# Which engines cut x into its two fp32r terms: ScalarE, VectorE and GpSimd by turns, or ScalarE and GpSimd alone

## The chip, the cores and the metric

The kernel runs on one core of a Trainium2 chip. The core has a matrix engine (TensorE), three engines for elementwise work (VectorE, ScalarE, GpSimd), an engine that issues transfers (SyncE) and DMA queues. Each engine works through its own list of instructions in order, and semaphores tie the lists together. The metric is device time in microseconds of one execution of the whole program. The profile is of one such execution: it gives each instruction's start, its duration, and what ended the idle time in front of it.

In the profile PE stands for TensorE's matmuls, PEld for its weight loads, DVE for VectorE, ACT for ScalarE, POOL for GpSimd and SP for SyncE.

## What is computed

Attention with a sliding window of 128 positions and a distance bias, and behind it a feed-forward layer:

```python
scores = scale * np.matmul(q, k.transpose(0, 1, 3, 2))       # 8 batches, 8 heads, 576 x 64
scores = np.where(mask, scores + bias[None], -1000000000.0)  # 0 <= row - column < 128
...
attn = np.exp(scores)
attn = attn / (np.sum(attn, axis=-1, keepdims=True) + 1e-09)
return np.matmul(attn, v).astype(np.float32)
...
x = np.ascontiguousarray(attn_out.transpose(0, 2, 1, 3)).reshape(B * S, H * D)   # 4608 x 512
h = x @ w_in                                                 # 512 x 2048
g = h * (1.0 / (1.0 + np.exp(-1.702 * h)))
return (g @ w_out).astype(np.float32)                        # 2048 x 512
```

Everything is float32. The matmuls of the feed-forward layer run in a reduced format, fp32r. To keep the precision, an operand a is cut into two fp32r terms, a rounded one (ah) and what is left (al = a - ah), and a product is made of three: ah bh + ah bl + al bh.

## The kernel before

The attention's output x is kept transposed, in chunks of T = 256 rows of the 4608, each a tile `xf` of 128 partitions x 4 quarters x 256 columns. There are 18 chunks. Chunks 0 to 11 are computed by objects of the class `Job`, one chunk each; chunk 0 is done in two jobs, for the first 8 blocks of 128 hidden columns and for the other 8, so there are 13 jobs. Chunks 12 to 17 are computed two at a time by objects of the class `Pair`, in another scheme of products, which does not use the function that is changed.

A job first calls `split_x` (L560), which makes the tiles `xh` (L564, rounding, as the cast of a copy) and `xl` (L566, subtraction), quarter by quarter: 4 roundings and 4 subtractions of 128x256 each. Rounding is on ScalarE for the chunks in `BESIDE`, which are 0 to 3 (5 jobs), and on VectorE for chunks 4 to 11 (8 jobs). The subtraction is on GpSimd for the even quarters and on VectorE for the odd ones. Both tiles have one buffer (the pool `xp` has bufs=1), so the split of the next job can write a tile only when the matmuls of the job before have read it.

Then, for each block f of 128 hidden columns, `Job.up(f)` (L580) runs 12 matmuls into `h_ps`, which has two buffers: 4 with `xh` and the weight's high term, 4 with `xh` and its low term, 4 with `xl` and the high term. Behind them come the tanh on ScalarE (L585), a product on VectorE that gives `g` (L586), its rounding on ScalarE (`gh`, L589) and the subtraction on GpSimd (`gl`, L590). `Job.down(f)` (L600) runs 6 matmuls of 512 columns into `acc`: two with each of `gh` and the two weight terms, and the last two with `gl`. The main loop over all blocks of all jobs calls, in each step, the decoding of weights that are still to come, the attention's ticks (`advance`), then `up` of the next block (through `begin`, with the split, if it is the first of a job), then `down` of this one.

The attention's units run beside it, in ticks. On GpSimd these have the subtractions for Q, K and V (L329, L330, L318), a sum (L551), and, in the first two batches, the normalisation `pb` (L420), for which the transposes of L438 wait. On ScalarE they have the roundings (L310, L328, L317), the exponentials (L399) and copies out of PSUM (L474, L548). In the first part of the program the weights come in and are decoded and cut too, on all three engines (L227 to L233), and sums of them are made and stored (L654 to L665).

The program's order is not the order of the source alone: the program is built with `schedule_with_timeline_sim=True`, so a planner lays out each engine's list by a timeline of its own when the program is built. On the chip each list then runs in that order.

Of the kernel before, what the change touches and what calls it, by code (L numbers as in the profile page):

```python
# [8 lines left out]
F32 = mybir.dt.float32  # L9
# [5 lines left out]
ALU = mybir.AluOpType  # L15
# [18 lines left out]
BIG = 3.0e38  # L34
FAR = 1.0e37
DEPTH = 3
BESIDE = range(4)
WB = 2
DECODE_TICKS = 5, 6, 7
FETCH_AHEAD = 6  # L40
# [113 lines left out]
def tile_kernel(ctx: ExitStack, tc: tile.TileContext, q0, k0, v0, qT, kT, v, w_in, w_out, out):  # L154
    nc = tc.nc
# [404 lines left out]
    def split_x(c, x):  # L560
        xh = xp.tile([P, NC, T], F32R, name="xh")
        xl = xp.tile([P, NC, T], F32R, name="xl")
        for k in range(NC):
            (nc.scalar.copy if c in BESIDE else nc.vector.tensor_copy)(xh[:, k], x[:, k])  # L564
            sub = nc.vector if k % 2 else nc.gpsimd
            sub.tensor_tensor(xl[:, k], x[:, k], xh[:, k].bitcast(F32), ALU.subtract)  # L566
        return xh, xl

    class Job:
# [330 lines left out]
    def begin(j):  # L900
        nonlocal seen
        recall(j.c)
        x = xf.pop(j.c)
        j.xh, j.xl = split_x(j.c, x)
        if j.f1 < NF:
            xf[j.c] = x
            send(j.c)
        seen = max(seen, j.c)
        recall(seen + 1)
        j.up(j.f0)  # L910
# [130 lines left out]
```

## Time and profile before

| | |
|---|---|
| time, median of 3 runs | 1059.15 us (1058.39 to 1060.15) |
| time of the profiled execution | 1062.32 us |
| its span, first to last instruction | 1060.5 us |
| mean granted TensorE clock | 0.988 of full speed |
| DMA traffic | 151.91 MB, 143 GB/s on average |
| the splits of x start at | 16, 89, 152, 186, 254, 313, 377, 439, 499, 562, 622, 684 and 744 us |

The span is what the profile's shares refer to. Matmuls are pipelined and their ends are modelled, so the start of one stands about 0.115 us (256 columns) behind the last although each is given as 0.28. A row of a timeline has the start, the time from the start to the end of a run of equal instructions, the engine, the line, the operation, output and inputs, the shapes, and the number of instructions. In square brackets stand the idle time before it and what ended that. A row of a view by groups has the number of instructions, their busy time, the mean time of one, and the idle time of the engine in front of them with what ended most of it.

### The profile page before, as it was taken

Reading aid. Unit: us, or ns where it says so; the run is one execution under the profiler, and the core shown is the slowest. Engines: PE = TensorE matmul, PEld = TensorE weight load, DVE = VectorE, ACT = ScalarE, POOL = GpSimd, SP = SyncE. Lnnn points to the kernel's source line nnn. Section 1 sums busy time; section 2 is a strip of 40 time slices with the busy share of each in tenths; the row PEclk is TensorE's granted clock in tenths of the full one; section 3 lists DMA queues with packets and bytes.
Section 4 is the critical chain, followed back from the end, with each engine's and each line's share of the span. In section 5 each row is a group of like instructions: output and inputs, shape, how many; then the busy total and the mean of one; then the engine's idle time right before and its main releaser. Section 6 shows DMA issues by size and latency. Waiting matters only on the chain.

```text
span 1060.5 us, 21877 instructions
## 1 busy us (share of the span) xinstructions
PE 1037.9 (98%) x6897; PEld 913.6 (86%) x6897; DVE 683.0 (64%) x2280; ACT 675.4 (64%) x1974; POOL 620.1 (58%) x832
## 2 busy tenths in 40 slices
PE   8889999999999999999999999999999999999998
PEld 5557878789998999999899999999988998898987
DVE  6877576357777787867778686776744345436343
ACT  6968876568777777777777777777633334335332
POOL 3668887457676677767677676766642233215121
PEclk9969999999999999999999999999999999999999
DMA  8975456333224234332423432342174556556551
GB/s 286 371 239 185 147 160 196 108 85 94 80 83 131 82 96 125 112 80 89 141 83 113 119 107 81 106 136 69 57 274 163 170 174 212 179 165 205 188 179 60
DMA packets 120276, 151.91 MB, mean 143 GB/s; under 512 B 40033, under 2 KB 96865, under 8 KB 120161
## 3 DMA queue, kind: packets, MB, share of 16 engines
q1 hardware_dynamic: 114400, 140.55, 42.6%
q10 hardware_dynamic: 5760, 9.96, 2.6%
q8 instruction: 55, 0.90, 0.4%
q14 instruction: 61, 0.49, 0.2%
HBM read 119.01 MB, written 31.46 MB: 142 GB/s over the span
## 4 chain that ended last, share of the span: by engine, by line
PE 79%; DVE 4%; issue 1%; DMA 1%; ACT 1%; POOL 0%; POOLq 0%; ACTq 0%; SPq 0%; DVEq 0%
PE acc L600 21%; PE h_ps L580 21%; PE accs L780 11%; PE X_ps L721 6%; PE s_ps L352 5%; PE x_ps L518 4%; PE Y_ps L721 4%; PE t_ps L461 4%; PE x_ps L495 1%; DVE xf L710 0%; DMA xf<-x 0%; PE t_ps L438 0%; DVE xh L564 0%; DMA part<-wc 0%; DVE xl L566 0%
## 5 line engine op out<-in xcount | busy, mean ns | idle before, releaser
L580 PE MATMUL h_ps<-xh,w 128*128 128x256 f32 x1536 | 251.5, 288 | 8.4 <-DVE g L586 7.5
L580 PEld LDWEIGHTS h_ps<-xh,w 128*128 128x128 f32 x1536 | 213.4, 190 | 26.9 <-issue 7.5
L600 PE MATMUL acc<-w,gh 128*128 128x512 f32 x768 | 220.8, 402 | 0.5 <-ACT g L585 0.4
L590 POOL TENSOR_TENSOR gl<-g,gh 128x256 fp32r<-128x256 f32 x192 | 147.1, 767 | 99.4 <-ACT gh L589 78.0
L733 POOL TENSOR_TENSOR gs<-g,gs 128x512 fp32r<-128x512 f32 x48 | 63.4, 1320 | 168.7 <-PE Y_ps L721 113.8
L780 PE MATMUL accs<-w,gs 128*128 128x512 f32 x576 | 148.3, 393 | 0.3 <-POOL gs L733 0.3
L600 PEld LDWEIGHTS acc<-w,gh 128*128 128x128 f32 x768 | 131.7, 190 | 18.2 <-ACT g L585 0.8
L330 POOL TENSOR_TENSOR K<-rk,K 128x384 fp32r<-128x384 f32 (+1 forms) x120 | 108.8, 907 | 50.7 <-ACT K L328 45.5
L580 PE MATMUL h_ps<-xl,w 128*128 128x256 f32 x768 | 137.2, 284 | 0.2 <-DVE xl L566 0.2
L600 PE MATMUL acc<-w,gl 128*128 128x512 f32 x384 | 127.3, 407 | 1.1 <-POOL gl L590 1.1
L780 PEld LDWEIGHTS accs<-w,gs 128*128 128x128 f32 x576 | 102.2, 189 | 17.7 <-POOL gs L733 0.7
L580 PEld LDWEIGHTS h_ps<-xl,w 128*128 128x128 f32 x768 | 112.4, 191 | 5.2 <-issue 0.6
L399 ACT ACTIVATE pb<-pb,mins 128x256 f32<-128x256 f32 (+2 forms) x216 | 104.6, 486 | 11.6 <-DVE mins L380 11.1
L586 DVE SCALAR_TENSOR_TENSOR g<-g,h_ps 128x256 f32<-128x256 f32 x192 | 79.5, 415 | 49.6 <-ACT g L585 48.1
L589 ACT CAST gh<-g 128x256 fp32r<-128x256 f32 x192 | 77.6, 405 | 50.2 <-DVE g L586 45.4
L585 ACT ACTIVATE g<-h_ps 128x256 f32<-128x256 f32 x192 | 72.7, 380 | 56.1 <-PE h_ps L580 45.9
L380 DVE CUSTOM_DVE_ANT_0 pb<-s_ps,bias 128x256 f32<-128x256 f32 (+3 forms) x240 | 86.0, 380 | 26.9 <-PE s_ps L352 24.7
L424 DVE TENSOR_SCALAR_CACHE_REDUCE pb<-pb,rec 128x256 f32<-128x256 f32 (+2 forms) x216 | 91.0, 454 | 3.2
L329 POOL TENSOR_TENSOR Q<-rq,Q 64x256 fp32r<-64x256 f32 (+1 forms) x120 | 83.0, 691 | 13.6 <-ACT Q L310 3.4
L480 DVE TENSOR_TENSOR pl<-t_ps,ph 128x512 fp32r<-128x512 f32 (+2 forms) x120 | 72.9, 607 | 16.0 <-ACT ph L474 14.1
L461 PE MATMUL t_ps<-ident,pb 128*128 128x128 f32 x408 | 80.8, 272 | 0.5 <-DVE pl L480 0.5
L328 ACT CAST K<-rk 128x384 fp32r<-128x384 f32 (+1 forms) x120 | 56.5, 471 | 29.4 <-PE s_ps L352 23.7
(116 smaller groups left out, 2057.8 us busy)
## 6 DMA issues: line engine op xcount, KB each, us to landing
ring<-part SPq DMA_DIRECT2D x84, 512.0 KB, 3.3
rk<-kT SPq DMA_DIRECT2D x72, 192.0 KB, 2.6
rq<-qT SPq DMA_DIRECT2D x96, 128.0 KB, 2.4
out<-o ACTq DMA_DIRECT2D x34, 256.0 KB, 2.8
rw<-w_in SPq DMA_DIRECT2D x16, 512.0 KB, 6.0
rw<-w_out SPq DMA_DIRECT2D x16, 512.0 KB, 6.8
x<-xf SPq DMA_DIRECT2D x13, 512.0 KB, 3.4
xf<-x SPq DMA_DIRECT2D x13, 512.0 KB, 4.4
```

Source lines behind the costliest of these rows:

```text
L329: nc.gpsimd.tensor_tensor(Q[D:], rq[D:], Q[D:].bitcast(F32), ALU.subtract)
L330: nc.gpsimd.tensor_tensor(K2, rk, K1.bitcast(F32), ALU.subtract)
L380: nc.vector.tensor_tensor_reduce(b.p[ra:rb, cs:b.end], u.s[ra:rb, e, cs:b.end], bias[head][ra:rb, cs:b.end], -SCALE, BIG, ALU.add, ALU.min ...
L399: nc.scalar.activation(live, live, AF.Exp, bias=u.mins[:b.rows, e:e + 1], scale=-1.0, accum_out=u.sums[:b.rows, e, :1],)
L424: nc.vector.tensor_scalar(live, live, u.rec[:rows, e:e + 1], None, ALU.mult, ALU.add, u.rec[:rows, 2 + e:3 + e])
L461: nc.tensor.transpose(u.t[:c.n, w:w + b.rows], b.p[:b.rows, col:col + c.n], ident[:b.rows, :b.rows])
L580: nc.tensor.matmul(h, w1[f][:, z, k * P:(k + 1) * P], x[:, k], start=(n == 0), stop=(n == len(ops) - 1))
L586: nc.vector.scalar_tensor_tensor(g, g, 1.0, h, ALU.add, ALU.mult)
L590: nc.gpsimd.tensor_tensor(gl, g, gh.bitcast(F32), ALU.subtract)
L600: products.append(nc.tensor.matmul(acc, g[:, t * P:(t + 1) * P], w2[f][:, z], start=(f == self.f0 and n == 0), stop=(f == self.f1 - 1 and ...
L721: nc.tensor.matmul(bank, w[:, z, k * P:(k + 1) * P], x[:, y, k], start=start and i == 0, stop=i == len(ops) - 1, skip_group_check=True)
L780: products.append(nc.tensor.matmul(self.acc[t], g[:, y, t * P:(t + 1) * P], w2[f][:, z], start=(f == 0 and n == 0), stop=(f == NF - 1 and ...
```

## The change

For every chunk, all four roundings are on ScalarE and all four subtractions on GpSimd. The five splits of chunks 0 to 3 (chunk 0 has two) had their roundings there already, so in these only the two odd subtractions move. In the eight splits of chunks 4 to 11 four roundings and two subtractions move.

```diff
-BESIDE = range(4)
...
         xh = xp.tile([P, NC, T], F32R, name="xh")
         xl = xp.tile([P, NC, T], F32R, name="xl")
         for k in range(NC):
-            (nc.scalar.copy if c in BESIDE else nc.vector.tensor_copy)(xh[:, k], x[:, k])
-            sub = nc.vector if k % 2 else nc.gpsimd
-            sub.tensor_tensor(xl[:, k], x[:, k], xh[:, k].bitcast(F32), ALU.subtract)
+            nc.scalar.copy(xh[:, k], x[:, k])
+            nc.gpsimd.tensor_tensor(xl[:, k], x[:, k], xh[:, k].bitcast(F32), ALU.subtract)
         return xh, xl
```

## What the change does to the time: the prediction

> **What bounds the kernel now.** I read the page first, then the busy time of stretches, then TensorE's own waits, then the two lines that change. The page, total and one group:
>
> ```profile
> span 1060.5 us, 21877 instructions
> ...
> PE 1037.9 (98%) x6897; PEld 913.6 (86%) x6897; DVE 683.0 (64%) x2280; ACT 675.4 (64%) x1974; POOL 620.1 (58%) x832
> ...
> L590 POOL TENSOR_TENSOR gl<-g,gh 128x256 fp32r<-128x256 f32 x192 | 147.1, 767 | 99.4 <-ACT gh L589 78.0
> ```
>
> TensorE is busy for 98% of the span and idle for 1060.5 - 1037.9 = 22.6 us. No other engine is above 64%. GpSimd mostly stands idle ahead of its most frequent job, `gl`, and waits there for ScalarE. But such shares are averages, so here are three stretches (busy us and instructions of each engine):
>
> ```profile
> core 0: us, PE busy (x) PEld busy (x) DVE busy (x) ACT busy (x) POOL busy (x), PEclk, DMA share, GB/s
> 16.00:89.00 73.00, 64.80 (x385) 44.30 (x383) 60.02 (x149) 54.66 (x162) 47.15 (x42) 0.86 0.91 313
> 89.00:100.00 11.00, 9.57 (x61) 7.79 (x60) 7.56 (x27) 9.35 (x31) 9.98 (x11) 1.00 0.22 73
> ...
> 313.00:745.00 432.00, 430.84 (x3028) 397.18 (x3027) 327.68 (x1347) 324.05 (x1001) 304.97 (x484) 1.00 0.36 104
> ```
>
> From 313 to 745 us, where eight of the thirteen splits of x lie (the last starts at its edge), TensorE is idle for 1.2 us of 432. There the three other engines have 24 to 29% of their time free. In the short stretch at 89 us, right behind the split of chunk 1, it is otherwise: GpSimd is busy for 9.98 of 11 us and TensorE loses 1.4. TensorE's waits, over the whole span (us, times, longest):
>
> ```profile
> PE h_ps L580 <- DVE g L586: 7.5, 4, 5.0
> PE t_ps L438 <- POOL pb L420: 2.9, 3, 1.9
> ...
> PE acc L600 <- POOL gl L590: 1.1, 1, 1.1
> ...
> PE h_ps L580 <- DVE xl L566: 0.2, 1, 0.2
> ```
>
> The split's own part in them is 0.2 us, once. So a quicker split has almost nothing to win directly, and the question is how much later the new one may be before TensorE feels it.
>
> **The change part by part.** The two lines, by form (count, busy us, mean ns, idle before), and then with least, median and longest ns:
>
> ```profile
> L566 POOL TENSOR_TENSOR xl<-xf,xh 128x256 fp32r<-128x256 f32 x26 | 21.4, 838 | 7.0 <-ACT xh L564 5.3 <-DVE xh L564 1.1 <-DVE rec L411 0.4
> ...
> L566 DVE TENSOR_TENSOR xl<-xf,xh 128x256 fp32r<-128x256 f32 x26 | 17.5, 691 | 1.0 <-ACT xh L564 0.8
> ...
> L564 DVE CAST xh<-xf 128x256 fp32r<-128x256 f32 x32 | 14.1, 495 | 1.2 <-PE h_ps L580 1.1
> ...
> L564 ACT CAST xh<-xf 128x256 fp32r<-128x256 f32 x20 | 6.9, 404 | 0.6 <-DVE xf L504 0.6
> ```
>
> ```profile
> L566 POOL TENSOR_TENSOR xl<-xf,xh x26: 726/839/975, 16.6 to 747.1; 128x256 fp32r<-128x256 f32 x26
> L566 DVE TENSOR_TENSOR xl<-xf,xh x26: 396/683/996, 20.4 to 746.6; 128x256 fp32r<-128x256 f32 x26
> ```
>
> ```profile
> L564 DVE CAST xh<-xf x32: 273/294/1241, 313.1 to 745.8; 128x256 fp32r<-128x256 f32 x32
> ...
> who waited for it (us, times):
> ...
>   PEld h_ps L580: 1.0, 2
> ```
>
> Load moves as follows. VectorE loses 32 roundings and 26 subtractions, 14.1 + 17.5 = 31.6 us. ScalarE gains 32 x 0.404 = 12.9 us. GpSimd gains 26 x 0.838 = 21.8 us, or 26 x 0.726 = 18.9 us if VectorE beside it no longer slows it. Nothing is issued to a DMA queue by these lines, and no number of bytes changes. The totals hide behind TensorE: GpSimd comes to 642 of 1060 us. What counts is the moment of each split.
>
> *Rounding, eight splits (chunks 4 to 11).* I look at the split at 377 us, the one with the least room:
>
> ```profile
> 378.11 0.46 POOL L318 TENSOR_TENSOR VV<-rv,VV 128x64 fp32r<-128x64 f32 x1
> 378.53 1.72 POOL L566 TENSOR_TENSOR xl<-xf,xh 128x256 fp32r<-128x256 f32 x2
> ...
> 383.57 0.74 POOL L590 TENSOR_TENSOR gl<-g,gh 128x256 fp32r<-128x256 f32 x1
> ```
>
> ```profile
> 377.14 1.58 DVE L564 CAST xh<-xf 128x256 fp32r<-128x256 f32 x4 [0.87 <-PE h_ps L580]
> ```
>
> ```profile
> 378.46 0.38 ACT L585 ACTIVATE g<-h_ps 128x256 f32<-128x256 f32 x1 [0.57 <-PE h_ps L580]
> ```
>
> ```profile
> 381.12 0.39 PE L580 MATMUL h_ps<-xl,w 128*128 128x256 f32 x2
> 381.38 0.49 PE L580 MATMUL h_ps<-xl,w 128*128 128x256 f32 x2
> ```
>
> ```profile
> 385.95 0.62 PE L600 MATMUL acc<-w,gl 128*128 128x512 f32 x2
> ```
>
> VectorE needs 1.58 us for the four roundings, and ScalarE took 1.32 us for four at 88.87 us (row below). ScalarE's queue gets up to 1.32 us in front of the tanh of L585. Behind that tanh stand `gh` (L589) and then GpSimd's `gl`. Here `gl` ends at 384.31 and is wanted at 385.95, which leaves 1.64 us, more than 1.32. VectorE's roundings stood in front of the same chain, at L586, and that delay goes. I take **0**. The gain cannot exceed the 1.0 us that weight loads waited for the roundings.
>
> *Subtraction, thirteen splits.* The two odd quarters now stand behind the two even ones in GpSimd's queue. With 0.84 us each, the last lands 1.68 us behind the present end of GpSimd's pair. At 377 us that is 378.53 + 1.72 + 1.68 = 381.93. TensorE takes the last quarter at 381.38 + 0.49 - 0.28 = 381.59 (0.28 being one matmul), so it would be 0.34 us late. The same sum for others, first and last of the thirteen among them:
>
> ```profile
> 30.66 0.40 DVE L566 TENSOR_TENSOR xl<-xf,xh 128x256 fp32r<-128x256 f32 x1
> 31.68 0.63 PE L580 MATMUL h_ps<-xl,w 128*128 128x256 f32 x4
> ```
>
> ```profile
> 88.87 1.32 ACT L564 CAST xh<-xf 128x256 fp32r<-128x256 f32 x4
> 89.35 1.81 POOL L566 TENSOR_TENSOR xl<-xf,xh 128x256 fp32r<-128x256 f32 x2 [0.88 <-ACT xh L564]
> ...
> 92.61 0.40 PE L580 MATMUL h_ps<-xl,w 128*128 128x256 f32 x2
> ```
>
> ```profile
> 684.57 1.57 POOL L566 TENSOR_TENSOR xl<-xf,xh 128x256 fp32r<-128x256 f32 x2 [0.50 <-DVE xh L564]
> ...
> 687.77 0.50 PE L580 MATMUL h_ps<-xl,w 128*128 128x256 f32 x3
> ```
>
> ```profile
> 746.26 1.79 POOL L566 TENSOR_TENSOR xl<-xf,xh 128x256 fp32r<-128x256 f32 x2
> ...
> 750.03 0.40 PE L580 MATMUL h_ps<-xl,w 128*128 128x256 f32 x2
> ```
>
> The first split gets x quarter by quarter, so its last subtraction merely takes 0.73 instead of 0.40 us: 31.39 against 31.68. At 89 us the landing is 92.84 against 92.73, 0.11 late. At 684 us it is 687.82 against 687.99, in time, and at 746 us 749.73 against 750.15, in time. Eleven of thirteen come in time in this way. The sum of what is late is 0.34 + 0.11, about **+0.5 us**.
>
> Behind these subtractions GpSimd's other jobs wait 1.5 us longer. At 377 us `gl` comes 3.3 us after the pair and has the 1.64 us of room. In the long stretch I take 0 for this. The full stretch at 89 us is another matter:
>
> ```profile
> 93.47 2.01 POOL L420 TENSOR_SCALAR pb<-pb,rec 128x128 f32<-128x128 f32 x2
> 96.02 1.52 POOL L420 TENSOR_SCALAR pb<-pb,rec 128x128 f32<-128x128 f32 x2 [0.54 <-ACT wh L660]
> ```
>
> Four subtractions alone, 4 x 0.73 = 2.9 us, replace a pair of 1.81: GpSimd gets 1.1 us more where 1.0 is free, and these `pb` rows are what the transposes of L438 wait for. Between 0 and +1.1 us I take the middle, **+0.5 us**.
>
> The Trainium skill, "GPSIMD Engine Reference", Engine selection, speaks against the move: two-input elementwise work belongs on VectorE, GpSimd being about twice as slow. The trace's least times agree, 726 against 396 ns. If that price fell on the path, the sum would be up to 26 x 0.33 = 8.6 us; rival B is its form here.
>
> **Sum:** 0 + 0.5 + 0.5 = +1.0 us. The profiled execution took 1062.3 us, 1.8 outside its span, and lies 3.2 above the median of 1059.15. Carried to the median, the forecast is **1060.2 us**. A difference under 0.2% (2.1 us) is about what a measurement of this kernel cannot tell from none, so I call this no change.
>
> **The rivals.**
>
> *A, the forecast:* the extra delay stays inside the room that TensorE's order already leaves. Chance 0.50.
>
> *B, GpSimd turns late at each split (slower).* If a `gl` of 0.77 us gets between the four subtractions, the last lands 2.45 us behind the present pair's end instead of 1.68. Against the four splits after the first quoted above, the room was 1.57, 1.34, 1.85 and 2.10 us, so TensorE would stall for 0.88, 1.11, 0.60 and 0.35, on average 0.74. It decides from about 1.5 us of lag on, the least room being 1.34. For the eight splits of the long stretch that is +5.9 us: 1059.15 + 5.9 = 1065.0. For it: the `VV` row directly in front of the pair, so that queue is not empty. Against it: TensorE's order is drawn up when the program is built and can put other work ahead. With all of GpSimd's added 21.8 us on the path it would be 1081, which the rooms above exclude. Chance 0.28.
>
> *C, the order is drawn anew.* The planner orders all engines' work by its own timeline. A first split that differs can shift everything behind it, above all from 16 to 89 us, where 73.00 - 64.80 = 8.2 of TensorE's 22.6 idle us lie. I estimate 4 us either way from the waits above (2.9 + 1.1 for GpSimd, 7.5 - 5.0 for VectorE): 1063 or 1055. Chance 0.08 slower, 0.06 faster.
>
> *D, VectorE's relief shows (faster).* The longest wait for `g`:
>
> ```profile
> 68.04 1.20 PE L580 MATMUL h_ps<-xh,w 128*128 128x256 f32 x4 [5.03 <-DVE g L586]
> ```
>
> VectorE's rounding took 273 ns at best and 1241 at worst, and its subtraction 396 to 996. If that friction also holds up `g` (L586), its end would win 2.5 us of the 7.5, since this one of 5.0 lies away from any split, and 0.2 for `xl`: 1059.15 - 2.7 = 1056.5. For it: the four waits for `g` are TensorE's dearest. Against it: the long stretch has only 1.2 idle us. Chance 0.08. The Trainium skill, "SBUF — State Buffer", Who interferes with whom, gives a reason: a VectorE copy in a two-port mode, or an operation with two SBUF inputs, and a GpSimd one lock each other out. The spread of the rows fits that; GpSimd's longer work, by the same rule, also holds up VectorE's other such operations more.
>
> **How the numbers follow.** Same 0.50 (A). Slower 0.28 + 0.08 = 0.36. Faster 0.06 + 0.08 = 0.14. The likeliest is A, 1060.2 us, with an own range of 1057.2 to 1061.2. The whole range goes from 1056.0, just under D, to 1067.0, two us above B, since B's 0.74 us could hold at more than eight splits.
>
> **What would show it.** In the changed profile: VectorE at about 651 us, ScalarE 688 and GpSimd 639 to 642; four roundings on ScalarE within about 1.3 us; four subtractions on GpSimd near 0.73 us each, the last 3 to 5 us after the first rounding; TensorE's idle time still under 24 us, and 313 to 745 us still nearly without it. Matmuls of `h_ps` waiting for POOL `xl` L566 at many splits, 0.3 to 1 us each, would show B. More than 2 us of difference before 254 us, at places without a split, would show C. The wait for `g` behind the split at 89 us gone would show D. The prediction is wrong if TensorE's total idle time moves by more than 2 us.

## The result, and the profile after

| | before | after |
|---|---|---|
| time, median | 1059.19 us (1058.39 to 1060.15, 4 runs) | 1053.91 us (1052.31 to 1054.14, 4 runs) |
| profiled execution, its span | 1062.32 us, 1060.5 us | 1052.31 us, 1050.5 us |
| mean granted TensorE clock in it | 0.988 | 0.997 |

The ratio is 0.9947, 95% interval 0.9929 to 0.9964: the changed kernel is 5.3 us faster (3.8 to 7.5). The forecast was no change, 1060.2 us, with a range that ended at 1056.0. It was wrong. The two profiles lie 10 us apart, about twice the difference of the medians, in part because before's was taken at a lower clock. How much of the 10 us that makes is worked out below. In the changed kernel, lines behind the split have numbers lower by 2 (L564 is now the subtraction, L584 is `g`), those ahead of it by 1.

The loads, from the page of the changed kernel (span, engines) and its groups by form (count, busy us, mean ns, idle before them):

```profile
span 1050.5 us, 21865 instructions
...
PE 1030.2 (98%) x6897; PEld 909.8 (87%) x6897; DVE 659.8 (63%) x2222; ACT 681.8 (65%) x2006; POOL 634.0 (60%) x858
```

```profile
L564 POOL TENSOR_TENSOR xl<-xf,xh 128x256 fp32r<-128x256 f32 x52 | 38.0, 763 | 4.4 <-ACT xh L563 3.9
...
L563 ACT CAST xh<-xf 128x256 fp32r<-128x256 f32 x52 | 17.5, 401 | 0.2
```

All 52 roundings are ScalarE's and all 52 subtractions GpSimd's, so the change does what it says. The loads came near the forecast: VectorE 659.8 against about 651, ScalarE 681.8 against 688, GpSimd 634.0 against 639 to 642.

Where the gain lies is read from stretches. "Start" below is the beginning of the first rounding of the split at 254 us, that of chunk 3, the last that is rounded by ScalarE in both kernels. "Rest" is from there to the end of the span. Per kernel, the first row is the rest and the second the 492 us behind the start, in which all later splits lie (columns as in the windows of before):

```profile
254.16:1060.50 806.34, 798.30 (x5388) 729.08 (x5387) 516.85 (x1791) 496.69 (x1428) 450.41 (x646) 1.00 0.42 129
254.16:746.16 492.00, 490.84 (x3454) 452.56 (x3454) 372.79 (x1532) 370.20 (x1142) 348.20 (x552) 1.00 0.35 102
```

```profile
247.73:1050.50 802.77, 796.72 (x5386) 728.66 (x5384) 493.70 (x1736) 502.40 (x1459) 457.96 (x662) 1.00 0.42 129
247.73:739.73 492.00, 492.00 (x3480) 455.35 (x3479) 352.93 (x1491) 379.27 (x1182) 358.77 (x573) 1.00 0.36 102
```

The first pair is before, the second after. The start comes 6.4 us earlier and the rest is 3.6 us shorter; together that is the 10.0 us. The granted clock is 1.00 in all four rows, so the 3.6 us are not the clock's. In 492 us from the start the changed kernel runs 3480 matmuls and the one before 3454, at 0.14 us each 3.7 us of work: the rest's whole gain is made among the eight splits of chunks 4 to 11. That is the stretch in which the prediction saw 1.2 idle us and nothing to win. The 6.4 us of the start are mostly another matter (experiments 6 and 12).

TensorE's own waits, over the whole span of the changed kernel (us, times, longest):

```profile
PE t_ps L437 <- POOL pb L419: 2.7, 3, 1.6
PE h_ps L578 <- DVE g L584: 1.7, 3, 0.9
...
PE h_ps L578 <- POOL xl L564: 0.7, 2, 0.4
PE acc L598 <- POOL gl L588: 0.6, 2, 0.4
```

The wait for `g` fell from 7.5 to 1.7 us. GpSimd's `xl`, which the prediction feared at 2 splits, is waited for twice, for 0.7 us.

What a split looks like is seen best at 499 us. In the kernel before, VectorE, then ScalarE, then TensorE (timelines):

```profile
499.39 1.83 DVE L564 CAST xh<-xf 128x256 fp32r<-128x256 f32 x3
...
502.04 0.84 DVE L564 CAST xh<-xf 128x256 fp32r<-128x256 f32 x1
502.80 0.41 DVE L566 TENSOR_TENSOR xl<-xf,xh 128x256 fp32r<-128x256 f32 x1
...
503.53 0.41 DVE L586 SCALAR_TENSOR_TENSOR g<-g,h_ps 128x256 f32<-128x256 f32 x1
...
508.25 0.68 DVE L480 TENSOR_TENSOR pl<-t_ps,ph 128x512 fp32r<-128x512 f32 x1
```

```profile
499.92 0.38 ACT L585 ACTIVATE g<-h_ps 128x256 f32<-128x256 f32 x1 [0.66 <-PE h_ps L580]
...
503.98 0.41 ACT L589 CAST gh<-g 128x256 fp32r<-128x256 f32 x1 [1.81 <-DVE g L586]
...
505.92 0.51 ACT L399 ACTIVATE pb<-pb,mins 128x256 f32<-128x256 f32 x1 [1.54 <-DVE mins L380]
```

```profile
502.93 0.65 PEld L580 LDWEIGHTS h_ps<-xh,w 128*128 128x128 f32 x5 [0.33 <-DVE xh L564]
...
508.99 0.33 PE L461 MATMUL t_ps<-ident,pb 128*128 128x128 f32 x1 [0.27 <-DVE pl L480]
```

The tanh ends at 499.92 + 0.38 = 500.30, but `g` starts only at 503.53, 3.2 us later: VectorE's list has most of the four roundings, a subtraction and a few short jobs of the attention ahead of it. ScalarE, which had no part in this split, then waits 1.81 us for `g` and 1.54 us for `mins`. TensorE's stall comes at 508.99, nearly 10 us behind the first rounding, for a tile of the attention. Only one wait here bears the name of the split, that of a weight load for the fourth rounding (0.33 us at 502.93). The same split in the changed kernel, ScalarE and VectorE:

```profile
491.52 1.33 ACT L563 CAST xh<-xf 128x256 fp32r<-128x256 f32 x4
492.87 0.39 ACT L583 ACTIVATE g<-h_ps 128x256 f32<-128x256 f32 x1
```

```profile
493.72 0.42 DVE L584 SCALAR_TENSOR_TENSOR g<-g,h_ps 128x256 f32<-128x256 f32 x1
```

Here the tanh ends at 493.26 and `g` starts 0.46 us later.

### The profile page after: what moved, and what is told of

Same layout as the page of the kernel before. It is cut to its first block, busy times and chain, and to the rows that moved or that the text cites. A ratio compares the mean times of both kernels' runs of the same rounds, so it can differ in the third digit from the quotient of the medians.

```text
span 1050.5 us, 21865 instructions
## 1 busy us (share of the span) xinstructions
PE 1030.2 (98%) x6897; PEld 909.8 (87%) x6897; DVE 659.8 (63%) x2222; ACT 681.8 (65%) x2006; POOL 634.0 (60%) x858
## 4 chain that ended last, share of the span: by engine, by line
PE 81%; POOL 2%; DVE 2%; issue 2%; ACT 1%; DMA 1%; POOLq 0%; SPq 0%; ACTq 0%; DVEq 0%
PE h_ps L578 22%; PE acc L598 22%; PE accs L778 11%; PE X_ps L719 6%; PE s_ps L351 5%; PE x_ps L517 5%; PE Y_ps L719 4%; PE t_ps L460 4%; POOL w L232 1%; PE x_ps L494 1%; DVE xf L708 0%; DMA xf<-x 0%; PE t_ps L437 0%; PE sb_ps L341 0%; POOL xT L701 0%
## 5 line engine op out<-in xcount | busy, mean ns | idle before, releaser
L598 PE MATMUL acc<-w,gh 128*128 128x512 f32 x768 | 217.1, 398 | 0.0
L584 DVE SCALAR_TENSOR_TENSOR g<-g,h_ps 128x256 f32<-128x256 f32 x192 | 79.5, 416 | 57.8 <-ACT g L583 52.4
L460 PE MATMUL t_ps<-ident,pb 128*128 128x128 f32 x408 | 78.0, 272 | 0.0
L351 PE MATMUL s_ps<-K,Q 128*128 128x256 f32 (+1 forms) x432 | 75.0, 287 | 0.0
```

Source lines behind the costliest of these rows:

```text
L351: nc.tensor.matmul(u.s[:b.rows, e, b.first:b.end], u.Q[:, b.q0 - u.q0:b.q0 - u.q0 + b.rows], k[:, ko:ko + b.end - b.first], start=(z == 0) ...
L460: nc.tensor.transpose(u.t[:c.n, w:w + b.rows], b.p[:b.rows, col:col + c.n], ident[:b.rows, :b.rows])
L598: products.append(nc.tensor.matmul(acc, g[:, t * P:(t + 1) * P], w2[f][:, z], start=(f == self.f0 and n == 0), stop=(f == self.f1 - 1 and ...
```

## The experiments

Two theories stood against each other. The first: the gain is made at the later splits, by VectorE's relief. The second: it is made in the first 250 us, or by a planner's list that happens to be better. Each kernel was timed beside the one before on one chip. The numbers together (start from ScalarE's timeline, the next three columns from the windows as above):

| kernel | median us (runs) | ratio to before, 95% | start | rest | of it TensorE idle | matmuls in 492 us |
|---|---|---|---|---|---|---|
| before | 1058.8 to 1058.9 | | 254.16 | 806.3 | 8.0 | 3454 |
| 1 early only | 1059.66 (12) | 1.0004, 0.9991 to 1.0017 | 248.91 | 809.0 | 9.6 | 3430 |
| 2 late only | 1056.93 (12) | 0.9973, 0.9959 to 0.9986 | 253.98 | 802.8 | 6.2 | 3481 |
| 3 first split only | 1061.48 (12) | 1.0019, 1.0005 to 1.0033 | 253.11 | 808.2 | 7.8 | 3448 |
| 4 first split swapped | 1062.06 (12) | 1.0028, 1.0011 to 1.0044 | 251.59 | 808.3 | 7.8 | 3448 |
| 5 the change again | 1053.12 (6) | 0.9937, 0.9917 to 0.9956 | 247.70 | 803.3 | 6.7 | 3480 |
| 6 late rounding only | 1054.15 (6) | 0.9947, 0.9928 to 0.9966 | 249.68 | 802.4 | 6.4 | 3481 |
| 7 late subtraction only | 1060.94 (12) | 1.0014, 1.0000 to 1.0029 | 251.62 | 807.0 | 8.3 | 3464 |
| 8 the change, idle sums | 1055.24 (6) | 0.9954, 0.9937 to 0.9972 | 247.84 | 805.3 | 7.0 | 3466 |
| 9 both halves | 1053.9 (6) | 0.9955, 0.9940 to 0.9969 | 247.67 | 803.4 | 7.5 | 3483 |
| 10 swapped early | 1057.72 (12) | 0.9986, 0.9974 to 0.9999 | 250.76 | 803.2 | 6.0 | 3479 |
| 11 twice the idle sums | 1055.7 (10) | 0.9965, 0.9954 to 0.9977 | 249.17 | 806.0 | 7.5 | 3464 |
| 12 late rounding again | 1055.79 (12) | 0.9979, 0.9964 to 0.9994 | 257.81 | 803.2 | 6.9 | 3481 |

The last column parts the kernels by one thing. The seven with all roundings on ScalarE and no sums (after, 2, 5, 6, 9, 10 and 12) get 3479 to 3483 matmuls done, and TensorE is drawn busy for all 492.00 us. The five with the late roundings on VectorE (before, 1, 3, 4 and 7) get 3430 to 3464 done. The seven have three different lists at the start and both ways of dividing the late subtractions, so a lucky list doesn't explain them.

**1 and 2, the two halves.** In 1 the odd subtractions of chunks 0 to 3 move and the rest is as before; in 2 chunks 4 to 11 are as in the change and chunks 0 to 3 as before.

```diff
 # 1
-sub = nc.vector if k % 2 else nc.gpsimd
+sub = nc.vector if k % 2 and c not in BESIDE else nc.gpsimd
 # 2
-(nc.scalar.copy if c in BESIDE else nc.vector.tensor_copy)(xh[:, k], x[:, k])
-sub = nc.vector if k % 2 else nc.gpsimd
+nc.scalar.copy(xh[:, k], x[:, k])
+sub = nc.vector if k % 2 and c in BESIDE else nc.gpsimd
```

> The five splits of chunks 0 to 3 are as in the changed kernel (all four subtractions on GpSimd), the eight of chunks 4 to 11 as before. Theory O (order): the gain is made at the start, because the order drawn anew no longer lets VectorE's shift (L228, 5.89 us at 61.7 us before) meet four GpSimd subtractions in a row; then this kernel is 4 to 6 us faster than before. Theory V (relief of VectorE): the gain follows the VectorE time taken away, of which these splits have 10 x 0.69 = 6.9 of 31.6 us; then it is 1 to 1.5 us faster.

> The five splits of chunks 0 to 3 are as before, the eight of chunks 4 to 11 as in the changed kernel. All lists are as before up to about 305 us. Theory O: within 1.5 us of before, and the profile shows the long VectorE shift near 61.7 us again, 4 to 6 us, with TensorE's wait of about 5 us for g. Theory V: these splits take 24.7 of the 31.6 us off VectorE, so it is 3.5 to 4.5 us faster.

The late half shortens the rest from 806.3 to 802.8 us, all that the change itself wins there, and its ratio lies below 1. The early half brings the start forward and loses that again: its rest is the longest of all, 809.0. What stops TensorE in it between 300 and 760 us (its waits):

```profile
PE x_ps L518 <- DVE xf L557: 1.4, 2, 1.0
PE h_ps L580 <- DVE g L586: 0.6, 1, 0.6
PE x_ps L518 <- ACT ph L474: 0.5, 1, 0.5
PE t_ps L461 <- DVE pl L480: 0.3, 1, 0.3
PE h_ps L580 <- DVE xl L566: 0.2, 1, 0.2
```

Of 3.0 us, 2.5 are for products of VectorE. In the same stretch the changed kernel has one wait of 0.2 us. So the two halves don't add up from their own ratios (+0.4 and -2.8 us make -2.4, not -5.3). Of the forecasts, only theory O's for the shift in 2 came true (it is 5.9 us long again). 1 was not faster, as both theories had it, and the 2.0 us of 2 lie between what the two gave.

**3 and 4, the first split.** In 3 only its two odd subtractions move; in 4 its odd ones are GpSimd's and its even ones VectorE's, so no work moves at all. `done` is empty in the first call alone.

```diff
 # 3
-sub = nc.vector if k % 2 else nc.gpsimd
+sub = nc.vector if k % 2 and (c or done) else nc.gpsimd
 # 4
-sub = nc.vector if k % 2 else nc.gpsimd
+sub = nc.vector if k % 2 == (0 if c == 0 and not done else 1) else nc.gpsimd
```

> Only the very first split (chunk 0, first job, 16 to 31 us) has its two odd subtractions on GpSimd, 0.8 us of VectorE time in all; everything else as before. Theory O: order behind it is drawn anew, so the time may change by several us although hardly any work moves; with the long shift gone 4 to 6 us faster. Theory V: under 0.5 us.

> Only in the very first split, GpSimd subtracts the odd quarters and VectorE the even ones: each engine has exactly the work of before. Theory O: the order is drawn anew by this too, so the time may move by 1 to 6 us either way, down if the longest L228 of the profile is under 2 us, and not if it is still over 4. Theory V: same as before within 0.5 us.

Both were slower, and nothing of the start's gain came from the first split. The long shift was gone in both (longest L228 1.5 us), which by theory O should have made them faster. Experiment 4 shows how far a list drawn anew can go: the same instructions on the same engines, two and two exchanged in the first 32 us, took 0.28% longer (0.11 to 0.44%, 3 us). In its profile the rest is 2.0 us longer, but it holds six matmuls more than that of before (5394 against 5388), some 0.8 us.

**5, 6 and 7, the late half taken apart.** 5 is the changed kernel again. In 6 only the roundings of chunks 4 to 11 move to ScalarE, in 7 only their odd subtractions to GpSimd.

```diff
 # 6
-(nc.scalar.copy if c in BESIDE else nc.vector.tensor_copy)(xh[:, k], x[:, k])
+nc.scalar.copy(xh[:, k], x[:, k])
 # 7
-sub = nc.vector if k % 2 else nc.gpsimd
+sub = nc.vector if k % 2 and c in BESIDE else nc.gpsimd
```

> The changed kernel unaltered, beside the parts of it on one chip. Both theories: 4 to 6 us faster than before; in its profile TensorE has no wait over 0.2 us that a VectorE or ScalarE instruction ends between 250 and 745 us.

> Only the roundings of chunks 4 to 11 go to ScalarE; all subtractions stay divided. Lists as before up to 305 us. Theory V (VectorE's list at the split holds up its next g, pl and xf, and with them TensorE, some us behind the split): 14.1 of the 24.7 us that late splits take off VectorE go, so it gains at least half of what both together gained (2.0 to 2.9 us), 1 to 2.9 us. Theory L (what counted was the subtraction, two on VectorE locked against two on GpSimd): within 1 us of before, and the waits at 503, 509 and 567 us stay.

> Only the two odd subtractions of chunks 4 to 11 go to GpSimd; the roundings stay on VectorE. Theory V: 0.5 to 1.5 us faster than before, as some of VectorE's list at the split goes. Theory L: the whole 2 to 3 us. If VectorE's roundings meet GpSimd's longer run of subtractions, they become longer than the 0.44 us that one takes on average before, and the gain is lost.

The roundings alone do it (6, first row), the subtractions alone don't shorten the rest (7, second row):

```profile
249.68:1052.10 802.42, 796.06 (x5388) 728.86 (x5387) 506.32 (x1759) 505.27 (x1460) 449.22 (x646) 1.00 0.42 129
```

```profile
251.62:1058.60 806.98, 798.64 (x5388) 728.98 (x5387) 508.01 (x1775) 496.16 (x1428) 459.14 (x662) 1.00 0.41 128
```

VectorE's total is nearly the same in both, 506 and 508 us, and the rest differs by 4.6. So it isn't VectorE's load over the stretch that counts but which work of it. Among the splits 7 does gain a little, 10 matmuls or 1.4 us by the table, but it loses more than that behind them; why is not shown. By its median it is 2.2 us slower than before, where both theories had it faster, and 6 is 4.6 us faster, more than either had forecast. The waits of 7 between 300 and 760 us are again mostly VectorE's (6 has none there):

```profile
PE h_ps L580 <- DVE g L586: 1.3, 2, 0.7
PE x_ps L518 <- ACT ph L474: 0.3, 1, 0.3
PE s_ps L352 <- DVE mins L380: 0.2, 1, 0.2
```

**8 and 11, VectorE's time given back without use.** The changed kernel, and in chunks 4 to 11 a sum by VectorE over each rounded quarter, which nobody reads: 32 sums of 0.41 us, 13.1 us, where the roundings had been 14.1. In 11 there are two sums for each quarter.

```diff
 nc.scalar.copy(xh[:, k], x[:, k])
+if c > 3:
+    nc.vector.tensor_reduce(xs[:, k:k + 1], xh[:, k].bitcast(F32), mybir.AxisListType.X, ALU.add)
```

> The changed kernel, and at each split of chunks 4 to 11 VectorE also adds up each of the four rounded quarters into a column that nobody reads, about 0.33 us each, 1.3 us per split: load on VectorE at the place of the old roundings that nothing waits for and that needs no port of GpSimd's. Theory V by load alone: 1 to 3 us slower than the changed kernel, with waits of TensorE for VectorE's results behind splits. If load alone isn't it, but that the split's own matmuls waited for VectorE, or its lock with GpSimd: within 1 us of the changed kernel.

> e8 with two useless sums of each late rounded quarter instead of one: 8 x 0.41 = 3.3 us of VectorE per split, where e8 had 1.6. If VectorE's list at the split is what counts, it is slower than e8 (1.8 us over the changed kernel) by at least as much again: 3.5 to 8 us over the changed kernel. If e8's loss was only another order, it lies within 1.5 us of e8.

The rest grows from 802.8 and 803.3 to 805.3 and then 806.0. Work on VectorE at the place of the roundings, without any result that is waited for, goes with 2 to 2.5 us of the 3.5. Twice as much adds only 0.7, far from double, so the price isn't proportional to the time spent, which I had not expected. By their medians 11 is 0.5 us over 8, and a difference under 1.5 us was set down beforehand as the mark of a mere other order. The rest of 11:

```profile
249.17:1055.20 806.03, 798.55 (x5386) 729.28 (x5384) 512.16 (x1800) 503.24 (x1459) 457.57 (x662) 1.00 0.41 128
```

Both lie outside the 802.4 to 803.4 us of the seven kernels above, so VectorE's time at a split may account for about two thirds, but that is not shown: the lists were drawn anew, and in 8 VectorE also stood idle for 1.6 us, at two sums, until ScalarE's rounding was there. Whether the price of the roundings is VectorE's time, that matmuls depend on them, or that VectorE and GpSimd stand in each other's way, no run here separates. Nor does one show why the sixteen subtractions that 6 leaves on VectorE cost nothing (rest 802.4) while sums do.

**9, both halves at their best.** If late subtractions on GpSimd cost something, dividing them again should help: the early half as in the change, the late one as in 6.

```diff
+nc.scalar.copy(xh[:, k], x[:, k])
+sub = nc.vector if k % 2 and c not in BESIDE else nc.gpsimd
```

> The start of the changed kernel (all four subtractions of chunks 0 to 3 on GpSimd, lists as there up to about 305 us) with e6's late part (roundings of chunks 4 to 11 on ScalarE, subtractions divided). If the two gains add, it is 5 to 7 us faster than before, at or up to 1 us under the changed kernel; its late part, from the end of TensorE's 190th us of work on, takes 792 to 794 us in the profile. If the late subtractions on GpSimd matter too, it is slower than the changed kernel by over 1 us.

Its rest is 803.4, its interval overlaps that of the change for the most part, and its 5.0 us are the lower end of the forecast. It is no better than the changed kernel, and late subtractions on GpSimd cost nothing that can be measured.

**10 and 12, the start.** 12 is 6 once more. 10 is 6 with odd and even exchanged in all of chunks 0 to 3, again without moving work.

```diff
 # 10
-sub = nc.vector if k % 2 else nc.gpsimd
+sub = nc.vector if k % 2 == (c not in BESIDE) else nc.gpsimd
```

> e6 (late roundings on ScalarE, subtractions divided), and in the splits of chunks 0 to 3 GpSimd takes the odd quarters and VectorE the even ones: each engine's work is that of e6, only the lists of the start are drawn anew. If the start's part of the gain is a matter of the order, this differs from e6 by 1 to 4 us in either direction; if it comes from less work on VectorE, it is as e6 within 1 us.

> e6 again, unaltered, to tell how far the same program repeats and to stand beside e9 and e10: 3.5 to 5.5 us faster than before; the half-clock time of its first 110 us may differ from e6's 6.8 us, and the time up to TensorE's 190th us of work with it by up to 4 us.

12 must be read first. It is the same program as 6, and its single runs go from 1053.30 to 1062.79 us. Its profile was the longest of these runs. The first 110 us of before, of 6, of 12 and of the changed kernel, in this order:

```profile
0.00:110.00 110.00, 96.70 (x588) 68.43 (x589) 80.34 (x230) 82.39 (x249) 68.25 (x74) 0.89 0.80 269
```

```profile
0.00:110.00 110.00, 94.27 (x615) 67.04 (x616) 85.55 (x240) 84.00 (x257) 72.38 (x78) 0.97 0.80 274
```

```profile
0.00:110.00 110.00, 96.01 (x559) 67.03 (x560) 78.48 (x228) 78.47 (x239) 66.63 (x71) 0.86 0.77 261
```

```profile
0.00:110.00 110.00, 96.38 (x617) 68.40 (x618) 86.39 (x241) 85.58 (x260) 78.74 (x83) 0.97 0.81 280
```

6 and 12 run the same list and get 615 and 559 matmuls done, at a granted clock of 0.97 and 0.86. Their starts are 249.68 and 257.81, and their rests 802.4 and 803.2. So the start of one profile says little by itself: two profiles of one program lie 8 us apart there, together with the clock. Only starts at an equal clock may be compared. The changed kernel and 6 have 0.97 both and lie 247.73 against 249.68, **2.0 us** apart. Kernels with 0.95 are 5 (247.70) and 1 (248.91) against 10 (250.76) and 4 (251.59), 1.9 to 3.9 apart in the same direction. If 2.0 us is the change's own part, some 4.4 of the 6.4 us between the profiles of before and after are the clock's. 10 doesn't reach the start of the changed kernel, so exchanging the engines in chunks 0 to 3 is not enough; its median lies 1.9 us above that of 12 and 3.6 above that of 6, which was timed on another chip.

## Why the prediction was wrong

The sum of the parts: about 2.0 us at the start (single profiles give 1.9 to 3.9) and 3.5 us in the rest come near the 5.3 us of the medians. The medians alone don't give the parts so well: 2, 6 and 12, which have the start of before and rests within 0.8 us, are 2.0, 4.6 and 3.1 us faster than before.

**The step that failed** is the rounding: "I take **0**. The gain cannot exceed the 1.0 us that weight loads waited for the roundings." It measured about -3.5 us (the rest of 806.3 us becomes 802.4 in 6 and 803.2 in 12, where nothing else moves). The bound looked at who waited for the split's own tiles. At a split TensorE still has other work laid out, so it hardly stops there. The delay goes on in VectorE's list to `g`, `pl`, `xf` and `mins`, and stops TensorE up to 10 us later under those names. That the roundings on VectorE cost this is shown by 6 and 12, and by the seven kernels against the five. That VectorE's time is most of it is suggested by 8 and put in doubt by 11. The chain from one to the other was read at the split of 499 us and in the waits, not shown link by link: the longest delay of `g` behind its tanh at each of the eight splits, added up from the timelines, is 18.4 us before and 1.0 after, but 9.6 in 6 and 9.2 in 7, of which one is quick and one is not. So the delay of `g` alone doesn't decide. What goes with the rest better is how long weight loads waited for VectorE's results in the 546 us from the start. In the kernel before:

```profile
PEld h_ps L580 <- DVE g L586: 1.4, 2, 1.2
PEld t_ps L461 <- DVE pl L480: 0.9, 2, 0.5
...
PEld h_ps L580 <- DVE xl L566: 0.4, 1, 0.4
PEld h_ps L580 <- DVE xh L564: 0.3, 1, 0.3
PEld t_ps L461 <- DVE pb L424: 0.2, 1, 0.2
```

These are 3.2 us, of which the split's own tiles `xl` and `xh` have 0.7. In the five kernels with the late roundings on VectorE the sum is 2.8 to 3.7 us, in 8 and 11 it is 1.6 and 1.7, and in the seven others 0.2 to 1.4 (9 has another 1.4 us whose end the profile doesn't tell).

**The 1.2 idle us from 313 to 745** were taken as a cap on what could be won there. They aren't one. A matmul is drawn 0.28 us long though the next may follow after 0.115, so a stall shows 0.165 us shorter than it is, and one below 0.165 us not at all. Over the rest, TensorE's idle time fell by 2.0 us (8.0 to 6.1), and its busy time for equal work by 1.6 (798.30 to 796.72).

**Subtraction late at 2 splits, +0.5 us:** the size came near, 0.7 us, but not where it was put, so that was luck. At 377 us, the split with the least room, nothing was late. The changed kernel there, GpSimd and TensorE:

```profile
372.82 2.83 POOL L564 TENSOR_TENSOR xl<-xf,xh 128x256 fp32r<-128x256 f32 x4
```

```profile
375.55 0.28 PE L578 MATMUL h_ps<-xl,w 128*128 128x256 f32 x1
```

Four subtractions take 2.83 us, as forecast, and the first matmul with `xl` stands at 375.55, when the last is nearly done. The new order has other matmuls ahead of it. The two late ones are both behind the split of chunk 1 (at 82 us now):

```profile
87.69 0.51 PE L578 MATMUL h_ps<-xl,w 128*128 128x256 f32 x2 [0.36 <-POOL xl L564]
...
90.31 0.50 PE L578 MATMUL h_ps<-xl,w 128*128 128x256 f32 x2 [0.38 <-POOL xl L564]
```

**The full stretch at 89 us, +0.5 us:** GpSimd is in fact full, but nothing of a cost is left over. Columns as before:

```profile
82.00:94.00 12.00, 10.36 (x62) 7.93 (x61) 9.76 (x31) 10.60 (x37) 11.87 (x13) 1.00 0.22 74
```

It is busy for 11.87 of 12 us and TensorE idle for 1.6, against 1.4 of 11 before. What was waited for there, `g` behind the split (1.15 us of the 7.5), is gone, as rival D had it, and the two waits above stand in its place.

**Rival B** (GpSimd late at each split) fell: two late matmuls instead of eight or more, and 9 against 5 shows no price. **Rival D** had the right mechanism in part, VectorE's relief, at 0.08 and -2.7 us. Its price was taken from the waits that bear the name `g`, and it looked for the gain at the places where these stood, not in the long stretch. **Rival C** is open for the start: more than 2 us before 254 us, at places without a split, was its mark, and 1.9 to 3.9 at an equal clock came, at which places was not read. What makes it is not settled. It needs the subtractions of chunks 0 to 3 on GpSimd (every kernel that has them starts at 247.7 to 249.2, every other at 249.7 or later), and not the first split's alone (3). VectorE's relief there and a luckier list both fit.

**The mark for being wrong**, TensorE's idle time moving by over 2 us, was met: 22.6 to 20.3.

## What to carry to other kernels

Before a step is costed at nothing because nobody waits for its tiles, follow the engine that runs it: what stands behind it in that engine's list, and who waits for that ten microseconds later. A share of free time on that engine (24% here) doesn't mean that the list has room at the moment of the step, and idle time drawn under pipelined matmuls is no cap on a gain. Compare parts of two profiles only at an equal granted clock, and give a list that a planner draws anew two or three microseconds of its own either way before a cause is named.

## What the runs showed of the hardware

VectorE can be shut out for a whole run of GpSimd's instructions. In the kernel before, around 62 us, VectorE and GpSimd:

```profile
61.67 5.89 DVE L228 TENSOR_SCALAR rw<-rw 128x512 int32<-128x512 int32 x1
```

```profile
61.18 1.20 POOL L420 TENSOR_SCALAR pb<-pb,rec 64x192 f32<-64x192 f32 x1
...
62.35 4.92 POOL L233 TENSOR_TENSOR w<-wc,w 128x512 fp32r<-128x512 f32 x4
```

A shift whose median is 427 ns takes 5.89 us and ends at 67.56, 0.3 us behind the last of five GpSimd instructions in a row. This is what TensorE's longest wait for `g` (5.0 us) was made of. The Trainium skill, "SBUF — State Buffer", Who interferes with whom, says of a VectorE operation in a two-port mode and a GpSimd one that whoever comes first holds the shared port pair for its whole instruction and the other is blocked. The trace doesn't tell the shift's mode, but it agrees and goes further, as the loser didn't get in between two instructions. In the changed kernel the shift's longest is 1.5 us, but the next operation of the decoding takes up to 4.9 us: the two together are busy for 58.6 us before and 60.0 after. And 3, 4 and 10 lost the long shift too and were not faster than their counterparts for it. So the longest wait in the list of waits was not where the time lay.

One program's profiles (6 and 12) had a granted clock of 0.97 and 0.86 in the first 110 us and took 1053.92 and 1062.79 us. These 8.9 us are more than the change is worth.
